# Moving a batch's first output product to the end of its step, and the transposes after it behind the second unit

## The chip, the cores and the metric

The kernel runs on one core of one Trainium2 chip. The metric is the time of the kernel on the device in microseconds (us), the median over runs; less is better. All data is 32-bit float.

## The reference, cut to what matters

```python
def _attn_ref(x, h):                       # x (8, 5696, 128), h (5696, 128)
    L = 2 * S
    Xf, Hf = np.fft.rfft(x, n=L, axis=1), np.fft.rfft(h, n=L, axis=0)
    return np.fft.irfft(Xf * Hf[None], n=L, axis=1)[:, :S, :]

def _moe_ref(x, phi, w1, w2):              # x (45568, 128), 32 slots, 8 experts
    logits = x @ phi
    d = softmax over tokens(logits);  slot_input = d.T @ x
    slot_out = per expert: relu(slot_input @ w1) @ w2
    c = softmax over slots(logits);   return c @ slot_out
```

So a long convolution by Fourier transforms, for 8 batches of 5696 tokens with 128 channels, and behind it a soft mixture of experts over all 45568 tokens.

## The kernel before, in words

The transform is split into small matrix products. **Stage a** (`stage_a`, L230) multiplies folded input by a table (L241), evicts with ScalarE (L243) and stores to the DRAM tensor `f` (L248). It comes in a "low" half once per step and a "high" half once per two steps. **Stage b** works on *units*: a unit loads a tile `gt` of `f` (L270), TensorE multiplies (`stage_b1`, L284) into the single PSUM tile `bt`, VectorE multiplies by the filter's transform (L304 twice, L312 twice) into `yf`, and one unit later `stage_b2` multiplies back (L327), ScalarE evicts (L332) and SyncE stores to `zm` or, for the last third of a batch, to `zr` (queued in `pending`, issued by `flush`). A batch has 12 units; steps of odd number have one, steps of even number two.

**Stage c** works on *pairs* T, four (`NQ`) to a batch, 32 in all. `load_main` and `load_rest` read a pair's `zc` (1 MB, from `zm`) and `zx` (512 KB, from `zr`) into one buffer. `stage_c1` multiplies `zc` (L412) and adds the product of `zx` (L417) in four PSUM banks; ScalarE copies two of them out (L420, L421), VectorE folds (L404, L405, twice each), GpSimd adds (L430, four times). `stage_c2` transposes the result (L439, four groups, each evicted by ScalarE, L441); `stage_c3` multiplies by phi (L448, evicted by L453); `column_max` takes the maximum. In the next odd step `stage_c4` and `stage_c5` transpose logits and weights (L475, L491; evictions L479, L482, L486, L494) and `softmax_exp` runs on VectorE, GpSimd and ScalarE (L500, L501, L504). In the even step after that `softmax_sum` (L509 to L512) and `dispatch` (L527, VectorE L532); `stage_c6` transposes the result (L551, L561, store to `c_t` L562).

The order on each engine is written out by hand in the loop over steps t (L631): what the loop calls first stands first in every engine's queue. PSUM has a ring of four banks (`bank`, L167) that stages a and c take in turn; `bt` and `bz` of stage b have a place of their own, one buffer each. All loads and stores of the loop are issued by SyncE in program order. They use eight semaphores in turn, so that an issue waits until the transfer that had its semaphore eight issues earlier has landed.

Odd steps: stage a low, **c1 of pair T, flush, loads of pair T+1**, unit, c4 of T-1, stage a high, c5 and exp of T-1. Even steps: stage a low, unit, softmax sum and dispatch of T-1, **c2 of T, c6 of T-2**, unit, c3 of T. The `zx` of a batch's first pair holds the product of the batch's last units, which are stored shortly before; its load is issued in the even step ahead of its c1 (`load_rest`, L697), other pairs load `zx` right behind `zc`. From step 72 on stage a has no more work. Behind step 80 the last pairs run without units, then the experts and the output.

Of the kernel before, what the change touches and what calls it, by code (L numbers as in the profile page):

```python
# [70 lines left out]
def kernel(  # L71
# [41 lines left out]
    NQ = NJ // 2  # L113
# [26 lines left out]
    def of_tokens(p):  # L140

        v = p[:, 0:1]
        return bass.AP(tensor=v.tensor, offset=v.offset,
                       ap=[v.ap[0], [TR, 4], [HP, 2], [1, MH]])
# [22 lines left out]
    def bank():  # L167
        rings.append(rings.pop(0))
        return rings[-1].tile([P, 512], F32, name="bank", tag="bank")
# [53 lines left out]
    def flush():  # L223
        while pending:
            pending.pop(0)()
# [140 lines left out]
    def load_main(T):  # L366
        if T >= NT:
            return
        b, j = divmod(T, NQ)
        t_ = zring.pop(0)  # L370
        zring.append(t_)
        zs[T] = t_
        n = 2 * CH
        nc.sync.dma_start(
            out=t_[0][:, :, :, :, :].rearrange("p h n c d -> p (h n c d)"),
            in_=zm[b].rearrange("o k r c d -> (o k) r (c d)")[:, j * n:(j + 1) * n].rearrange(
                "p r x -> p (r x)"))

    def load_rest(T):
        if T >= NT:  # L380
            return
        b, j = divmod(T, NQ)
        t_ = zs[T]
        n = 2 * CH
        nc.sync.dma_start(
            out=t_[1][:, :, :, :].rearrange("p h n d -> p (h n d)"),
            in_=zr[(b + 1) % 2].rearrange("o c k r d -> (o c k) r d")[:, j * n:(j + 1) * n].rearrange(
                "p r x -> p (r x)"))
# [5 lines left out]
    def stage_c1(T, between=lambda: None):  # L394
        zt, zx = zs.pop(T)
        y_ = ybufs.pop(0)
        ybufs.append(y_)

        def part(v, f):
            k = (2 * v + f) * CH  # L400
            return y_[:, k:k + CH, 0:D] if f == 0 else y_[:, k + CH - 1:k - 1:-1, 0:D]

        def fold_out(even, minus, plus):
            nc.vector.tensor_tensor(out=plus, in0=even, in1=minus, op=AL.add)  # L404
            nc.vector.tensor_tensor(out=minus, in0=even, in1=minus, op=AL.subtract)  # L405

        ps = {(o, c): bank() for o, c in ((0, 1), (1, 0), (0, 0), (1, 1))}
        for c in (1, 0):
            for h_ in range(2):
                for o in range(2):  # L410
                    r = slice(o * HP, (o + 1) * HP)
                    nc.tensor.matmul(ps[o, c][h_ * HP:(h_ + 1) * HP, :], im[r, c, :],  # L412
                                     zt[r, h_, :, c, :], start=True, stop=False)
        for h_ in range(2):
            for (o, c), p in ps.items():
                r = slice((2 * o + c) * HALF, (2 * o + c) * HALF + N1 - MAIN)
                nc.tensor.matmul(p[h_ * HP:(h_ + 1) * HP, :], ir[r, :], zx[r, h_, :, :],  # L417
                                 start=False, stop=True)
        ps = {k: p[:, :].rearrange("p (n d) -> p n d", d=D) for k, p in ps.items()}
        nc.scalar.activation(part(0, 0), ps[0, 1], AF.Copy)  # L420
        nc.scalar.activation(om[:, :, :], ps[1, 0], AF.Copy)  # L421
        fold_out(ps[0, 0], part(0, 0), part(1, 0))
        a_ = ps[1, 1]
        between()

        def after():
            fold_out(a_, om[:, :, :], op[:, :, :])
            for v, o_, eng in ((1, op, nc.gpsimd), (0, om, nc.vector if tail else nc.gpsimd)):
                for part_, sign in ((part(v, 1), AL.subtract), (part(v, 0), AL.add)):
                    eng.tensor_tensor(out=part_, in0=part(v, 0), in1=o_[:, :, :], op=sign)  # L430

        ys[T] = y_
        return after

    def stage_c2(T):
        for k in (3, 1, 0, 2) if tail else (3, 2, 1, 0):
            p = bank()
            for i in range(CH):
                nc.tensor.transpose(p[:, i * TR:(i + 1) * TR], ys[T][0:TR, k * CH + i, 0:D],  # L439
                                    ident[0:TR, 0:TR])  # L440
            nc.scalar.activation(yt[:, k * CH:(k + 1) * CH, :, :], of_tokens(p), AF.Copy)  # L441
# [55 lines left out]
    def softmax_exp(T):  # L497
        rm = cpool.tile([P, Q * CH], F32, name="rm", tag="rm", bufs=1)
        Lv = Ls[T][:, :, :, :].rearrange("p k i s -> p (k i) s")
        nc.vector.reduce_max(out=rm[:, :], in_=Lv, axis=AX.X)  # L500
        nc.gpsimd.tensor_tensor(out=Lv, in0=Lv,  # L501
                                in1=rm[:, :].unsqueeze(2).broadcast_to([P, Q * CH, NSL]),
                                op=AL.subtract)
        nc.scalar.activation(Lv, Lv, AF.Exp)  # L504
# [98 lines left out]
    def units(t):  # L603
        g, i = divmod(t - LAG_B, NJ)
        if t < LAG_B or g > B:
            return []
        return [g * NW + k for k in range(sum(PER[:i]), sum(PER[:i + 1]))]
# [23 lines left out]
    for t in range(last_front + 1):  # L631
        us = list(units(t))

        def pair(lag):
            T, half = divmod(t - LAG_C - lag, 2)
            return T if half == 0 and 0 <= T < NT else None

        def prefetch(last):
            nonlocal loaded
            while loaded < len(queue) and queue[loaded][0] <= last \  # L640
                    and queue[loaded][0] // NW * NJ + NJ <= t:
                load_g(queue[loaded][0])
                loaded += 1

        def slot_b(due=True):
            fresh = due and bool(us)
            if fresh:
                u = us.pop(0)
                stage_b1(u)
                prefetch(u + AHEAD)  # L650
                wait_b2.append(u)
            if len(wait_b2) > fresh:
                stage_b2(wait_b2.pop(0))

        T, U, V, W, X = [pair(k) for k in (0, 2, 1, 3, 5)]
        if t < NA:
            stage_a(t, False)
            fold(t + 1)
        if t == last_front:
            assert T is None and U is None  # L660
            assert pair(-1) % NQ
            flush()
            dispatch(W)
            for i in range(3):
                slot_b()
                flush()
                if i == 1:
                    softmax_sum(W)
                    stage_c2(V)
            assert not us and not wait_b2  # L670
            stage_c6(X)
            stage_c3(V)
            column_max(V)
            break
        if t % 2:
            if T is not None:
                stage_c1(T)()
            flush()
            if pair(-2) is not None:
                load_main(pair(-2))  # L680
                if pair(-2) % NQ:
                    load_rest(pair(-2))
            slot_b()
            if U is not None:
                stage_c4(U)
            if t < NA:
                stage_a(t, True)
            if U is not None:
                stage_c5(U)
                softmax_exp(U)  # L690
            flush()
        else:
            if t % NJ == 0:
                prefetch(wait_b2[-1] + AHEAD if wait_b2 else AHEAD - 1)
            if t < NA:
                load_x(t // 2 + 2)
            if pair(-1) is not None and pair(-1) % NQ == 0:  # L697
                load_rest(pair(-1))
            flush()
            slot_b()  # L700
            if W is not None:
                softmax_sum(W)
                dispatch(W)
            flush()
            if V is not None:
                stage_c2(V)
            if X is not None:
                stage_c6(X)
            slot_b()
            if V is not None:  # L710
                stage_c3(V)
                column_max(V)
            flush()
        if t == NA:
            lead.close()
            wts = inner.enter_context(tc.tile_pool(name="wts", bufs=1, side="right"))
            w1s = wts.tile([P, E, F], F32, name="w1s")
        if NA < t <= NA + E:
            nc.sync.dma_start(out=w1s[:, t - NA - 1, :], in_=moe_w1[t - NA - 1])
# [3 lines left out]
    T = V + 1  # L723
# [209 lines left out]
```

## Time and profile before

| | |
|---|---|
| three runs, us | 912.71, 910.75, 908.36; median 910.75 |
| span of the profiled execution, first to last instruction | 906.7 us |
| busy: TensorE (PE) | 757.3 us, 84% |
| busy: VectorE (DVE) / ScalarE (ACT) / GpSimd (POOL) | 601.1 / 436.6 / 399.9 us |
| DMA moved | 278.33 MB, mean 307 GB/s |

The profile gives the span of one execution; its time outside the first and last instruction is not shown, and the median of the runs lies 4.05 us above the span. In the timelines below, the columns are start (us from the span's start), length in us, engine, line, operation, output and inputs, shape, count; in brackets the idle time of the engine just before it and what ended it. PE lengths overlap: the time that a group costs is the distance to the next group's start.

### The profile page before, as it was taken

The numbers are of one execution on the slowest core, as the hardware profiler recorded it, in microseconds if no ns is written. First come the engines' busy times: TensorE is split into PE (matmuls) and PEld (weight loads), VectorE is DVE, ScalarE is ACT, GpSimd is POOL, SyncE is SP. The second block draws the span as 40 slices with busy tenths as digits, with TensorE's granted clock in tenths as the row PEclk, the third lists the DMA queues.
The fourth block names the chain that finished last, engine by engine and source line by source line (L and its number), as shares of the span: only waits on it lengthen the run. The fifth ranks groups of instructions, "written<-read, shape, count | busy, mean of one in ns | idle before, by whom it ended". The sixth has DMA issues, their size and how long they took to land.

```text
span 906.7 us, 21292 instructions
## 1 busy us (share of the span) xinstructions
PE 757.3 (84%) x8308; PEld 383.0 (42%) x8308; DVE 601.1 (66%) x896; ACT 436.6 (48%) x880; POOL 399.9 (44%) x353
## 2 busy tenths in 40 slices
PE   5867687689989998998999999989888877767893
PEld 2222233234444443444444444435444434344882
DVE  2049876567778776777677787758778766653552
ACT  2423343345655565565556555645544444563441
POOL 4634424245656655655555566645332224651000
PEclk9889999989999999999899999989988888766865
DMA  8999999999999999999999999999988868540798
GB/s 264 314 312 342 321 362 290 307 369 357 320 298 375 347 322 337 353 315 291 360 354 331 312 366 348 324 329 331 294 252 293 267 199 341 186 164 1 296 405 332
DMA packets 170443, 278.33 MB, mean 307 GB/s; under 512 B 13543, under 2 KB 128231, under 8 KB 165135
## 3 DMA queue, kind: packets, MB, share of 16 engines
q1 hardware_dynamic: 169336, 275.74, 89.7%
q8 instruction: 66, 1.08, 0.5%
q10 hardware_dynamic: 1008, 1.25, 0.4%
q14 instruction: 33, 0.27, 0.1%
HBM read 147.94 MB, written 129.00 MB: 305 GB/s over the span
## 4 chain that ended last, share of the span: by engine, by line
PE 41%; DMA 32%; DVE 7%; ACT 7%; issue 6%; POOL 3%; SPq 2%; DVEq 0%; ACTq 0%; POOLq 0%
DMA gt<-f 9%; PE bt L284 8%; PE bank L241 7%; PE bz L327 7%; DMA zx<-zr 5%; DMA zc<-zm 5%; PE bank L412 4%; DMA out_dram<-o 4%; DMA f<-fst 4%; PE bank L417 3%; PE bank L439 3%; PE bank L448 2%; DMA zr<-zst 2%; ACT zst L332 2%; ACT fst L243 2%
## 5 line engine op out<-in xcount | busy, mean ns | idle before, releaser
L241 PE MATMUL bank<-x,s 128*32 128x512 f32 (+1 forms) x1152 | 216.5, 613 | 13.3 <-POOL x L217 8.2
L217 POOL TENSOR_TENSOR x<-xc 128x512 f32<-128x512 f32 x144 | 180.5, 1279 | 96.3 <-PE bank L241 77.8
L430 POOL TENSOR_TENSOR y<-y,op 128x512 f32<-128x512 f32 x64 | 77.6, 1212 | 227.6 <-DVE op L404 225.1
L284 PE MATMUL bt<-gt,wt 64*64 64x256 f32 x1620 | 123.3, 414 | 55.2 <-issue 27.1
L243 ACT ACTIVATE fst<-bank 128x512 f32<-128x512 f32 x216 | 123.0, 592 | 77.1 <-PE bank L241 53.5
L304 DVE TENSOR_TENSOR pi<-bt,Hi 128x1024 f32<-128x1024 f32 x96 | 112.9, 1176 | 65.1 <-PE bt L284 65.0
L332 ACT ACTIVATE zst<-bz 128x1024 f32<-128x1024 f32 x96 | 93.3, 972 | 109.8 <-PE bz L327 93.7
L312 DVE TENSOR_TENSOR yf<-bt,pi 128x512 f32<-128x512 f32 x192 | 119.3, 663 | 3.3
L284 PEld LDWEIGHTS bt<-gt,wt 64*64 64x64 f32 x1620 | 57.7, 140 | 135.7 <-issue 77.1
L304 DVE TENSOR_TENSOR bt<-bt,Hr 128x1024 f32<-128x1024 f32 x96 | 113.0, 1177 | 0.0
L327 PE MATMUL bz<-yf,vt 64*64 64x256 f32 x1440 | 109.3, 403 | 0.0
L241 PEld LDWEIGHTS bank<-x,s 128*32 128x32 f32 (+1 forms) x1152 | 54.0, 125 | 129.2 <-issue 91.3
L404 DVE TENSOR_TENSOR y<-bank,y 128x512 f32<-128x512 f32 x32 | 22.1, 692 | 97.2 <-ACT y L420 96.9
L327 PEld LDWEIGHTS bz<-yf,vt 64*64 64x64 f32 x1440 | 63.6, 143 | 25.4 <-issue 4.2
L512 POOL TENSOR_TENSOR L<-L,rs 128x512 f32<-128x512 f32 x32 | 33.5, 1048 | 87.2 <-DVE rs L511 43.7
L439 PE MATMUL bank<-ident,y 109*128 109x109 f32 x512 | 62.6, 272 | 8.8 <-ACT yt L441 8.8
L504 ACT ACTIVATE L<-L 128x512 f32<-128x512 f32 x32 | 20.2, 630 | 102.6 <-POOL L L501 102.6
L430 POOL TENSOR_TENSOR y<-y,om 128x512 f32<-128x512 f32 x54 | 63.9, 1183 | 2.1
L420 ACT ACTIVATE y<-bank 128x512 f32<-128x512 f32 x32 | 19.1, 596 | 93.0 <-PE bank L417 93.0
L439 PEld LDWEIGHTS bank<-ident,y 109*128 109x128 f32 x512 | 52.6, 148 | 20.4 <-POOL x L217 16.4
L412 PE MATMUL bank<-zc,im 64*64 64x512 f32 x480 | 60.8, 623 | 0.0
L441 ACT ACTIVATE yt<-bank 128x360 f32<-128x360 f32 x128 | 53.0, 483 | 6.2 <-PE bank L439 5.8
(101 smaller groups left out, 861.7 us busy)
## 6 DMA issues: line engine op xcount, KB each, us to landing
gt<-f SPq DMA_DIRECT2D x99, 512.0 KB
f<-fst SPq DMA_DIRECT2D x144, 240.0 KB
zm<-zst SPq DMA_DIRECT2D x128, 256.0 KB
zc<-zm SPq DMA_DIRECT2D x30, 1024.0 KB
xc<-in_x_dram SPq DMA_DIRECT2D x32, 768.0 KB
f<-fst SPq DMA_DIRECT2D x144, 120.0 KB
out_dram<-o SPq DMA_DIRECT2D x16, 1024.0 KB
zx<-zr SPq DMA_DIRECT2D x30, 512.0 KB
```

The lines of the kernel that those rows point to most:

```text
L217: nc.gpsimd.tensor_tensor(out=y_[:, o, :, :], in0=near, in1=far, op=AL.subtract if o else AL.add)
L241: nc.tensor.matmul(p[i * m:(i + 1) * m, :], s1[:, g // B, q + o, cols], columns(c_, o), start=True, stop=True)
L243: nc.scalar.activation(st[:, :, q, :], p[:, :].rearrange("p (n d) -> p n d", d=D), AF.Copy)
L284: nc.tensor.matmul(bt[q * HP:(q + 1) * HP, a, o, :], wt[r, 2 * i + q, :], t_[r, 2 * o + q, :, :].rearrange("p c d -> p (c d)"), start=True ...
L304: nc.vector.tensor_tensor(out=p_, in0=pv, in1=h_, op=AL.mult)
L312: nc.vector.tensor_tensor(out=y_[r, 0:k, c, :], in0=pv[:, :, c, :], in1=pi[r, 0:k, 1 - c, :], op=op_)
L327: nc.tensor.matmul(bz[a * HP:(a + 1) * HP, q, o, :], vt[r, i, a, :], y_[r, a * m + o, :, :].rearrange("p c d -> p (c d)"), start=True, sto ...
L332: nc.scalar.activation(st[:, 0:m, 0:n, :].rearrange("p o q x -> p q o x"), bz[:, 0:n, 0:m, :], AF.Copy)
L412: nc.tensor.matmul(ps[o, c][h_ * HP:(h_ + 1) * HP, :], im[r, c, :], zt[r, h_, :, c, :], start=True, stop=False)
L430: eng.tensor_tensor(out=part_, in0=part(v, 0), in1=o_[:, :, :], op=sign)
L439: nc.tensor.transpose(p[:, i * TR:(i + 1) * TR], ys[T][0:TR, k * CH + i, 0:D], ident[0:TR, 0:TR])
L441: nc.scalar.activation(yt[:, k * CH:(k + 1) * CH, :, :], of_tokens(p), AF.Copy)
```

## The change

For the first pair of each batch (T a multiple of 4; pairs 0, 4, ..., 24 fall into the loop over steps), c1, the flush behind it and the loads of the next pair go to the end of the odd step. For the same pairs, c2 and the c6 that stands with it go behind the even step's second unit.

```diff
         if t % 2:
-            if T is not None:
-                stage_c1(T)()
-            flush()
-            if pair(-2) is not None:
-                load_main(pair(-2))
-                if pair(-2) % NQ:
-                    load_rest(pair(-2))
+            late = T is not None and T % NQ == 0
+
+            def begin():
+                if T is not None:
+                    stage_c1(T)()
+                flush()
+                if pair(-2) is not None:
+                    load_main(pair(-2))
+                    if pair(-2) % NQ:
+                        load_rest(pair(-2))
+
+            if late:
+                flush()
+            else:
+                begin()
             slot_b()
             if U is not None:
                 stage_c4(U)
...
                 stage_c5(U)
                 softmax_exp(U)
+            if late:
+                begin()
             flush()
...
             flush()
-            if V is not None:
+            late = V is not None and V % NQ == 0
+            if V is not None and not late:
                 stage_c2(V)
-            if X is not None:
+            if X is not None and not late:
                 stage_c6(X)
             slot_b()
+            if late:
+                stage_c2(V)
+                if X is not None:
+                    stage_c6(X)
             if V is not None:
                 stage_c3(V)
                 column_max(V)
```

## The prediction

> **What bounds the kernel now.** The waits come first: who stood still for whom (total, times, longest, in us).
>
> ```profile
> PEld bank L417 <- DMA zx<-zr: 25.3, 6, 7.4
> PE bank L417 <- DMA zx<-zr: 20.0, 6, 6.5
> ```
>
> TensorE waits six times for `zx`, 20.0 us in all (the first row sees the same waits at the weight loads). By the rows of L417 they stand at pairs 0, 4, 8, 12, 16 and 20: 6.50, 2.27, 2.81, 3.79, 0.69 and 3.92 us; pair 24 waits for nothing. Next the chain that ended last, in the stretch ahead of pair 12's wait (start, us, what):
>
> ```profile
> 417.11 8.31 DMA gt<-f
> 425.43 0.32 SPq L225
> ...
> 426.29 6.58 DMA zx<-zr
> ...
> 432.92 2.01 PE bank L417 x16
> ```
>
> SyncE stood until a `gt` load had landed, because a store needed its semaphore; only then came `zx`, though TensorE had begun that step at 414.41. So the wait is that of a late, full queue. The table by stretches shows how full (length; busy us of PE, PEld, DVE, ACT, POOL; granted clock; DMA share, GB/s):
>
> ```profile
> 262.00:344.00 82.00, 76.27 (x888) 36.57 (x880) 62.54 (x97) 46.83 (x96) 47.07 (x40) 1.00 1.01 341
> 680.00:740.00 60.00, 46.83 (x554) 26.24 (x553) 47.93 (x73) 25.07 (x50) 19.28 (x17) 0.83 0.82 272
> ```
>
> While stage a runs, DMA is busy throughout and TensorE nearly so: two near-equal bounds. Last, the even step behind pair 8, all engines:
>
> ```profile
> 357.08 1.10 PE L284 MATMUL bt<-gt,wt 64*64 64x256 f32 x16 [0.29 <-DVE yf L312]
> 358.00 1.04 PE L327 MATMUL bz<-yf,vt 64*64 64x256 f32 x16
> 358.97 1.09 PE L527 MATMUL bank<-y,d 128*32 128x129 f32 x32
> 360.00 1.34 PE L439 MATMUL bank<-ident,y 109*128 109x109 f32 x12
> 361.80 0.56 PE L439 MATMUL bank<-ident,y 109*128 109x109 f32 x4 [0.47 <-ACT yt L441]
> 362.20 0.54 PE L551 MATMUL bank<-ident,L 109*128 109x109 f32 x4
> 362.67 1.09 PE L284 MATMUL bt<-gt,wt 64*64 64x256 f32 x16
> ```
>
> ```profile
> 358.25 1.22 DVE L304 TENSOR_TENSOR pi<-bt,Hi 128x1024 f32<-128x1024 f32 x1 [0.62 <-PE bt L284]
> ...
> 360.64 1.29 DVE L312 TENSOR_TENSOR yf<-bt,pi 128x512 f32<-128x512 f32 x2
> ```
>
> Between the two units stand 5.6 us (357.08 to 362.67); VectorE needs 4.85 of them (to 361.93) before `bt` is free. The transposes now moved away are the cover of that work.
>
> **What each first pair cost before.** From one L412 to the next pair's: 27.0, 22.5, 23.0, 26.2, 20.9, 26.3 and 20.4 us for pairs 0 to 24. Less its wait, pairs 4, 8 and 16 come to 20.2; pairs 12 and 20 to 22.4, since behind 3.8 and 3.9 us of idleness L417 took 2.01 us, not 1.11, and L284 and L327 were as slow: 2.2 us at a lower clock. Waits of 2.27, 2.81 and, at 171.26, 2.99 left it alone. The Trainium skill (TensorE: Matmul & The Clock Gate, Part 1) says that an idle window of about 3.4 us halves the clock; these rows agree. By that rule the waits added below, 2.0 us at most in a regular pair, cost no clock.
>
> **The odd step.** A is the end of the low product, 344.13 for pair 8, where L412 started. Unit, c4, high product and c5 now come first: 1.89 + 0.59 + 1.85 + 0.59 us (349.94 to 354.86). The unit must wait for VectorE, whose unit before ends at 344.49: **+0.4**, new, because c1 no longer stands between. Then L412, 1.9. L417 comes at A + 7.2 instead of A + 1.9; `zx` landed at A + 2.5 to A + 5.8 for pairs 4 to 20, so the five waits go. Pair 0 has no c4 and c5: L417 could start at 181.7, `zx` lands at 183.4, 1.7 remain. In c1, TensorE waits for the second low eviction before; afterwards for c5's (L494 ends 1.3 after c5 starts), the same within 0.1. The exponential L504 now stands ahead of L420, but its GpSimd step L501 no longer stands behind L430; it ends at about A + 7.7, L420 starts at A + 8.3: nothing.
>
> **The even step.** The low product needs the bank that L420 empties (350.06 + 0.60, TensorE free at 349.94): **+0.75**; this eviction lay beside the unit before. The folds (L404, L405, 2.8 us) lie beside the low product and end before the first unit's L304 is due. First unit, back product and dispatch take 0.92 + 0.97 + 1.03 = 2.9 us; the second unit needs `bt`, free 4.85 behind the first one's start: **+2.0**. The y that c2 needs is ready: L430 ends 4.8 us behind the second fold, earlier than c2's new place. Behind c2 there is only c6 to cover ScalarE: the eviction L332 (1.03) and four L441 (1.70) end 2.75 us behind c2's start, c2 and c6 take 1.8 + 0.47: c3 waits **+0.5**. The waits of 0.29 and 0.47 above go. Sum 0.4 + 0.75 + 2.0 + 0.5 - 0.76 = **+2.9**, and a first pair costs 20.2 + 2.9 = 23.1 us. Nothing of it hides: TensorE's idle time in these stretches is these waits.
>
> **Pair 24** runs without stage a. Its unit waits 2.2 us for VectorE, its second even unit about 4.3, since the folds come right ahead of the first unit's multiplications; a wait of 2.28 goes. That makes +2.3 at full clock, +4.3 at the lower one that these steps showed before; I take +3.
>
> **TensorE's sum**, pairs 0 to 24: to 24.4 (-2.6), +0.6, +0.1, -3.1, +2.2, -3.2, +3.0: -3.0 us.
>
> **The loads of the next pair.** `zc` and `zx` of T+1 now stand behind a `gt` load, two `zm` stores and four `f` stores in SyncE's queue. In a pair whose c1 came on time:
>
> ```profile
> 457.10 0.52 SPq L374 DMA_DIRECT2D zc<-zm  x1
> 457.79 0.80 SPq L385 DMA_DIRECT2D zx<-zr  x1
> 458.68 0.43 SPq L270 DMA_DIRECT2D gt<-f  x1
> 459.77 1.79 SPq L225 DMA_DIRECT2D zm<-zst  x2
> 461.66 3.61 SPq L225 DMA_DIRECT2D f<-fst  x4
> 467.59 0.34 SPq L198 DMA_DIRECT2D xc<-in_x_dram  x1
> ```
>
> The seven took 8.9 us (458.68 to 467.59), part of it waiting for landings; their 1.5 MB are 4.5 us at 334 GB/s. No row shows the order itself, so `zc` comes 4.5 to 8.9 us later; I take 6, near the 6.6 to the last store's end. `zc` of pairs 1, 5, 9, 13, 17 and 21 landed 6.7, 6.1, 5.9, 8.4, 6.1 and 9.6 us before its L412 (landing: last update of the load's semaphore). With the pair lengths changed as above, 4.1, 6.7, 6.0, 5.3, 8.3 and 6.4 remain: a delay of 6 leaves waits of 1.9 and 0.7, **+2.6**; 4.5 leaves 0.4, 8.9 leaves 16.6. `zx` follows 1.3 us behind `zc` and is wanted 1.9 later: nothing. The next input load waits behind both, but its fold is not due for a step.
>
> **Sum**: -3.0 + 2.6 = -0.4 us on a span of 906.7; with the 4.05 us between span and median, **910.4 us**. A measurement can tell about 0.5%, 4.55 us, from no change.
>
> **Rivals.**
>
> *DMA sets the batch* (no change, 910.7). `zx` landed at 183.4, 265.8, 348.8, 432.9, 515.9 and 600.1: 82.4 to 84.1 us apart, whatever TensorE lost in between, and the DMA share is 1.00. Then the moved product doesn't free the loop: TensorE runs ahead until `zc` stops it. With landings kept and `zc` 6 us later, L412 of pair 21 comes 3.1 us earlier than before, pair 24 gives 3 back. Against it: SyncE also stood for compute, 12.5 us in 10 waits for L284. The Trainium skill (DMA: Bandwidth & Descriptors, Specifications) puts a core's share of HBM at about 358 GB/s, close above the 341 here, which would speak for this rival; but slices of this trace reach 405, so it is no ceiling here.
>
> *The later loads decide* (slower). If `zc` comes 8.9 us later and DMA has no lead to give, the waits at six L412 are 16.6: +13.6 us, 924.4. It decides from a delay of about 7.3 (8.0 us of waits, +5.0). For it: the seven issues did take 8.9. Against: two of those waits were for `zc` and `zx` themselves.
>
> *Half the price* (faster). If the second unit's wait and c3's come to half, because evictions and VectorE's order fit better than rows of another order show, 1.25 us go from each of seven pairs: -9.2 us, 901.6. Against: the 4.85 us of VectorE have stood behind every unit.
>
> **Chances.** Forecast 0.50, DMA 0.17, later loads 0.20, half price 0.13. So faster 0.13, within 0.5% 0.67, slower 0.20. The range: downwards no `zc` waits and pair 24 at +2.3 (907.1), and part of the half price: 905; upwards the forecast with `zc` about 8.0 later (11.5 us of waits, +8.5): 919. That leaves out the ends of the two outer rivals.
>
> **What would show it.** L417 of pairs 4 to 20 without a wait for `zx`, pair 0 with under 2 us; L284 of the even step behind waiting about 2 us for L312, L448 about 0.5 for L441, the low L241 about 0.75 for L420; L327 to L439 adjacent; no 1112 ns matmuls at pairs 12 and 20; L412 of pairs 1 and 13 waiting a little for `zc`. A wait over 2 us at most of the L412 behind would prove the second rival, `zx` waits at the new place the first, second-unit waits under 1 us the third.

## The result and the profile after

The changed kernel takes 918.08 us (median of 7 runs, 914.73 to 919.38), the kernel before, run beside it, 912.03: a ratio of 1.0064, 95% interval 1.0037 to 1.0091. It is slower, by about 6 us, where 0.4 us less was forecast. Measured once more on another chip, beside 26 runs of the kernel before (908.98), it gave 914.64 and 1.0069 (1.0042 to 1.0096). The ratios leave out the runs that lie over 1.5% above the fastest of their kernel; the medians hold all runs.

The profiled execution has a span of 917.6 us and took 919.38, so 1.8 us lie around the span. The kernel before's profiled span of 906.7 therefore belongs to a run of about 908.4, below its median of 912.03: the two spans, 10.9 us apart, overstate the change. 1.6 us of that are there before step 27, ahead of the first edit.

The waits of TensorE for the loads of stage c, whole execution; the first two rows are those shown of the kernel before:

```profile
PEld bank L417 <- DMA zx<-zr: 14.1, 9, 3.6
PE bank L417 <- DMA zx<-zr: 5.9, 6, 2.7
...
PE bank L412 <- DMA zc<-zm: 0.5, 2, 0.3
```

From 20.0 us the waits at L417 fell to 5.9 (pairs 0, 12, 16, 20: 2.70, 1.21, 0.71, 0.78; the rest at 9 and 13). So the change takes away most of these waits. The even step behind pair 8, where the price was to lie, with TensorE's low product ahead of it:

```profile
357.31 1.94 PE L241 MATMUL bank<-x,s 128*64 128x512 f32 x8 [0.79 <-ACT y L420]
359.18 1.09 PE L284 MATMUL bt<-gt,wt 64*64 64x256 f32 x16
360.10 1.04 PE L327 MATMUL bz<-yf,vt 64*64 64x256 f32 x16
361.07 1.09 PE L527 MATMUL bank<-y,d 128*32 128x129 f32 x32
364.13 1.09 PE L284 MATMUL bt<-gt,wt 64*64 64x256 f32 x16 [1.97 <-issue]
365.02 1.07 PE L327 MATMUL bz<-yf,vt 64*64 64x256 f32 x16
366.02 1.71 PE L439 MATMUL bank<-ident,y 109*128 109x109 f32 x16
367.58 0.59 PE L551 MATMUL bank<-ident,L 109*128 109x109 f32 x4
368.67 0.81 PE L448 MATMUL bank<-yt,phi 128*32 128x360 f32 x8 [0.50 <-ACT yt L441]
```

Three new waits: 0.79 for ScalarE's eviction, 1.97 ahead of the second unit, 0.50 ahead of c3. The second is marked "issue", but VectorE's row shows whose it is: its two L312 start at 362.74 and take 1.29, to 364.03. A fourth, 0.38, stands ahead of the odd step's unit at 348.39. The bracketed waits of 0.29 and 0.47 of before are gone.

The stretches and the chain ahead of pair 12's wait, as shown of before:

```profile
262.00:344.00 82.00, 75.92 (x860) 37.33 (x860) 61.93 (x95) 46.73 (x96) 44.62 (x39) 0.98 0.98 327
680.00:740.00 60.00, 45.26 (x572) 26.45 (x564) 45.32 (x70) 25.73 (x53) 18.89 (x17) 0.87 0.81 268
```

```profile
423.65 8.05 DMA gt<-f
431.72 0.32 SPq L225
...
432.57 7.90 DMA zx<-zr
...
440.51 1.19 PE bank L417 x16
```

In the first stretch the granted clock is 0.98, where it was 1.00, and DMA moves 327 GB/s, not 341. The chain is the same one, 6.3 to 6.5 us later, and its `zx` load takes 7.90 us instead of 6.58. The queue behind pair 8's product, in the new order:

```profile
359.33 0.38 SPq L270 DMA_DIRECT2D gt<-f  x1
359.98 1.54 SPq L225 DMA_DIRECT2D zm<-zst  x2
361.81 2.48 SPq L225 DMA_DIRECT2D f<-fst  x4
364.40 0.35 SPq L374 DMA_DIRECT2D zc<-zm  x1
365.72 0.35 SPq L385 DMA_DIRECT2D zx<-zr  x1
```

The seven issues ahead of `zc` took 5.1 us (359.33 to 364.40); `zc` landed at 371.34, and L412 started at 371.48.

The measure for what follows is the length of a *batch*: from L412 of pairs 1, 5, 9, 13, 17 and 21, whose place the change leaves alone, to the L412 four pairs on, in each profile (us):

| kernel | 1 | 5 | 9 | 13 | 17 | 21 | sum |
|---|---|---|---|---|---|---|---|
| before | 82.1 | 83.0 | 86.2 | 80.9 | 86.3 | 79.7 | 498.2 |
| changed | 84.0 | 83.6 | 85.3 | 84.9 | 84.3 | 83.7 | 505.8 |
| changed, second chip (after_same) | 84.0 | 83.2 | 84.4 | 83.2 | 84.6 | 85.9 | 505.3 |
| forecast by TensorE's sum | 82.7 | 83.1 | 83.1 | 83.1 | 83.1 | 82.7 | 497.8 |

The last row is the prediction's 23.1 us for the first pair (20.36 + 3 for pair 24), and for the other three pairs what they took before (59.6, four times 60.0, 59.37).

### The profile page after: what moved, and what is told of

It reads as the page before. It is cut to its first block, busy times and chain, and to the rows that moved or that the text cites. A ratio compares the mean times of both kernels' runs of the same rounds, so it can differ in the third digit from the quotient of the medians.

```text
span 917.6 us, 21233 instructions
## 1 busy us (share of the span) xinstructions
PE 751.2 (82%) x8308; PEld 381.8 (42%) x8308; DVE 604.9 (66%) x896; ACT 438.5 (48%) x880; POOL 399.7 (44%) x353
## 4 chain that ended last, share of the span: by engine, by line
PE 39%; DMA 32%; issue 8%; ACT 8%; DVE 6%; POOL 5%; SPq 1%; ACTq 0%; DVEq 0%; POOLq 0%
DMA gt<-f 10%; DMA zx<-zr 10%; PE bank L241 8%; PE bt L284 8%; PE bz L327 6%; PE bank L412 4%; DMA out_dram<-o 4%; DMA f<-fst 3%; PE bank L417 3%; POOL y L430 3%; PE bank L439 2%; PE bank L448 2%; ACT fst L243 2%; DMA zc<-zm 2%; ACT zst L332 2%
## 5 line engine op out<-in xcount | busy, mean ns | idle before, releaser
L241 PE MATMUL bank<-x,s 128*32 128x512 f32 (+1 forms) x1152 | 218.0, 616 | 19.8 <-POOL x L217 8.2
L284 PE MATMUL bt<-gt,wt 64*64 64x256 f32 x1620 | 121.7, 409 | 71.5 <-issue 41.8
L312 DVE TENSOR_TENSOR yf<-bt,pi 128x512 f32<-128x512 f32 x192 | 119.4, 663 | 3.3
L284 PEld LDWEIGHTS bt<-gt,wt 64*64 64x64 f32 x1620 | 58.3, 139 | 150.9 <-issue 79.0
L241 PEld LDWEIGHTS bank<-x,s 128*32 128x32 f32 (+1 forms) x1152 | 55.5, 125 | 138.2 <-issue 97.8
L412 PE MATMUL bank<-zc,im 64*64 64x512 f32 x480 | 60.6, 618 | 0.6 <-DMA zc<-zm 0.5
L501 POOL TENSOR_TENSOR L<-L,rm 128x512 f32<-128x512 f32 x32 | 33.6, 1049 | 55.0 <-DVE rm L500 54.0
```

The costliest lines, as they stand in the source:

```text
L241: nc.tensor.matmul(p[i * m:(i + 1) * m, :], s1[:, g // B, q + o, cols], columns(c_, o), start=True, stop=True)
L284: nc.tensor.matmul(bt[q * HP:(q + 1) * HP, a, o, :], wt[r, 2 * i + q, :], t_[r, 2 * o + q, :, :].rearrange("p c d -> p (c d)"), start=True ...
L312: nc.vector.tensor_tensor(out=y_[r, 0:k, c, :], in0=pv[:, :, c, :], in1=pi[r, 0:k, 1 - c, :], op=op_)
```

## The experiments

Ratios are to the kernel before, run beside the variant on the same chip, with 95% intervals. The kernel before itself lies between 907 and 912 us from chip to chip, so ratios or batches are compared, not medians of different chips.

**One half of the change at a time.** The edit is `late = False` in the even step (c1_only) or in the odd step (c2_only).

> First part alone: c1 and the next pair's loads of a first pair at the end of the odd step, c2 and c6 at their old place. TensorE's own price per first pair by rows of the changed kernel: 0.4 (unit behind VectorE) + 0.75 (low product behind L420) + about 0.4 (c2's last group behind L430) - 0.3 = 1.25 us, not 2.9. Theory 'TensorE's own sum' (what the product is moved past costs, and zx lands early enough): 7 x 1.65 = 11.5 us faster than the changed kernel, about 906, with no zx wait. Theory 'DMA sets the pace' (the loads of zx land every 84 us whatever TensorE does): 2 to 5 us faster than the changed kernel, 911 to 916, with zx waits of 1 to 2 us back at the moved L417.

> Second part alone: c1 as before, c2 and c6 of a first pair behind the second unit. TensorE's own price per first pair: 2.0 (second unit behind VectorE) + 0.5 (c3 behind L441) - 0.76 = 1.7 us. 'TensorE's own sum': 7 x 1.7 = 12 us slower than before, about 924, with the zx waits of the kernel before (20 us in all) unchanged. 'DMA sets the pace': the next zx wait gives the 1.7 us back, so that only the first pairs without a wait pay: +2 to +5 us, 914 to 917, and the zx waits fall to some 10 us.

c1_only: 911.48 us, 1.0024 (0.9991 to 1.0057), no clear difference, where TensorE's own sum had expected a gain of some 5 us. Its waits of over 0.4 us for `zx` fell to pairs 1, 9 and 20, but `zc` of pairs 5, 9, 13, 17 and 21 came late by 1.55, 0.45, 1.13, 1.56 and 1.27 us. c2_only: 922.16 us, 1.0146 (1.0098 to 1.0194), as TensorE's own sum had it:

```profile
PE bank L417 <- DMA zx<-zr: 14.8, 6, 4.0
```

Its `zx` waits fell by only 5 us (from 20.0), so the added work was not given back at the next wait. The second part is the costly one.

**The price without DMA in the way.** In `load_x` each row's length becomes a quarter; these kernels leave out three quarters of the input's columns:

```diff
-                                ap=[v.ap[0], [(a[1] - a[0]) * D, 2], [1, n * D]])
+                                ap=[v.ap[0], [(a[1] - a[0]) * D, 2], [1, n * D // 4]])
                     nc.sync.dma_start(
-                        out=t_[r0:r1, :, :, :].rearrange("p s n d -> p s (n d)"), in_=v)
+                        out=t_[r0:r1, :, 0:n // 4, :].rearrange("p s n d -> p s (n d)"), in_=v)
```

> The kernel before with only a quarter of each input load (x is left out for three quarters of the columns, which stay zero), 18 MB less of 278; all else in place. 'DMA sets the pace': 2.3 MB less a batch are 6.9 us at 334 GB/s, so zx comes in time, its waits fall under 5 us in all and a batch to TensorE's own 80.2 us: 15 to 22 us faster than before, 890 to 897. 'TensorE's own sum' with a zx whose lateness is the latency of store and load behind the last unit: waits stay above 10 us, 3 to 8 us faster.

> The changed kernel with the same quarter of each input load. No zx or zc wait is left, so the price on TensorE stands alone: 'DMA sets the pace' expects 15 to 20 us above before_light (7 x 2.9, less what zx waits were left there), 908 to 914. 'TensorE's own sum' expects 3 to 8 us above before_light, as with full loads.

> c1_only with the quarter input loads of the light kernels (x is left out for three quarters of the columns): no DMA wait is left, so the price of the first part stands alone. TensorE's own sum: 1.25 us for each of six pairs, some 2 for pair 24, against before_light's 883.7: 892 to 895; so 11 to 14 us below after_light's 905.9, which is the price of moving c2 and c6. If the price lies in the moved c1 instead, c1_light is within 5 us of after_light.

before_light: 883.65 us, 0.9716 (0.9674 to 0.9758). Its waits:

```profile
PE bank L417 <- DMA zx<-zr: 2.2, 3, 1.0
```

c1_light: 889.57, 0.9760 (0.9716 to 0.9805). after_light: 905.88, 0.9982 (0.9956 to 1.0008), with no `zx` or `zc` wait of over 0.1 us (c1_light has one, 0.94 for `zc` at pair 13). before_light and after_light ran on one chip: where hardly a load is late the change costs 22.2 us, against 20.3 (7 x 2.9) by the sum. c1_light ran on another, so the split is rougher: by the medians 5.9 us are the first part's and 16.3 the second's, by the ratios (of 907.37) 4.0 and 20.1, by the sums of the six batches (480.4, 490.9, 505.0) 10.5 and 14.1. Each way the second part is the larger.

Both light kernels lie beyond what 'DMA sets the pace' expected (before_light 24 us below the kernel before, not 15 to 22; after_light 22 above before_light, not 15 to 20), and far from the 3 to 8 us of the other theory. So in the kernel before it is the volume of the loads that makes `zx` late; what the moved work costs is TensorE's own, as in c2_only, where the added time was not given back.

The batches of after_light are 84.0, 83.1, 84.5, 84.4, 83.2 and 85.8; the first five of c1_light lie between 81.2 and 82.5, those of before_light between 79.8 and 81.2. Two of after_light's first five are as forecast, the other three 1.3 to 1.4 longer, and the last is 3 us longer. That pointed at the clock.

**The clock.** Three products of 128x64 by 128x512 without a reader stand in the wait ahead of the second unit:

```diff
+            if late and t < NA:
+                p = bank()
+                for _ in range(3):
+                    nc.tensor.matmul(p[0:HP, :], ident[:, 0:HP],
+                                     wt[:, 0:8, :].rearrange("p n r -> p (n r)"),
+                                     start=True, stop=True)
             slot_b()
```

> after_light with three extra products of 128x64 by 128x512 (about 0.47 us each; their result is not read) in the even step of pairs 0 to 20, in the wait ahead of the second unit; x is left out for three quarters of the columns as in after_light. If the 2.0 us of idleness there is what lowers the clock behind it in some pairs (1.3 us each in three of five batches of after_light), the granted clock stays at 1 there, all batches from pair 1 to pair 21 take 83.1 us instead of 83.1 to 84.5, and the time falls by 3 to 5 us from after_light's 905.9. If idleness there is not the cause, the extra products change nothing or cost up to 1.4 us a pair.

904.63 us, 0.9931 (0.9904 to 0.9958). Batches 83.7, 83.8, 83.8, 83.9, 83.8: the long ones are gone and all are alike, but the three products take 2.7 us, 0.7 more than the wait, so that the batches are no shorter on average. By times this would settle little (medians 905.88 and 904.63 of two chips, ranges overlapping); the rows do.

**The order of the loads.** In before_zx_first and after_zx_first, `load_rest` of the even step stands ahead of `load_x`. In before_zr_zx_first, also the 1 MB load of `zc` of a first pair stands behind its step's unit and the flush that stores `zr`. In after_loads_first, `begin` issues the loads ahead of the stores:

```diff
                 if T is not None:
                     stage_c1(T)()
-                flush()
+                if not late:
+                    flush()
                 if pair(-2) is not None:
                     load_main(pair(-2))
```

> The kernel before with the load of a first pair's zx ahead of the input load in the even step, not behind it. If the place in SyncE's queue and the 768 KB ahead of it make zx late, it lands about 2 us earlier (768 KB at 334 GB/s are 2.3 us): zx waits 20 to about 8 us, no low clock behind them, 8 to 12 us faster, 900 to 904. If DMA as a whole sets the pace, the input load lands that much later and the wait moves to other loads: within 3 us of before.

> As before_zx_first, and in the odd step ahead of it the stores of the batch's last unit (zr) stand ahead of the 1 MB load of zc, not behind it, so that zx need not wait for them. Queue order: zx lands some 4 us earlier, no wait for it, but zc comes 2 us later than its slack of 4 to 6 us: 15 us faster, about 897. DMA as a whole: within 4 us of before.

> The changed kernel with zx ahead of the input load. Its remaining zx waits (5.5 us in all) go: 3 to 6 us faster than the changed kernel, 912 to 915. If DMA as a whole sets the pace, the time stays that of the changed kernel, 918, and gt or zc waits take their place.

> The changed kernel with the next pair's loads ahead of the six stores that the end of the odd step issues. zc of pairs 9, 13, 17 and 21 lands 3 to 5 us earlier and their waits (1.7 us in all) go: 1 to 2 us faster than the changed kernel, if the later stores delay nothing. If DMA as a whole sets the pace: no change, 918, zx of the next batch waits longer instead. If SyncE, which now has to wait for c1 ahead of the stores, is what matters: 3 us or more slower.

before_zx_first: 911.33, 1.0028 (0.9997 to 1.0059): nothing gained. L417's waits for `zx` fell to 16.2 us, but units now waited 13.3 us for `gt`, where it had been 6.1:

```profile
PE bt L284 <- DMA gt<-f: 13.3, 8, 4.5
```

before_zr_zx_first: 904.44, 0.9941 (0.9904 to 0.9978), faster, though less than by queue order alone. after_zx_first: 919.98, 1.0104 (1.0056 to 1.0152). (No trace reading rests on these two.) after_loads_first: 916.17, 1.0094 (1.0063 to 1.0125). In its trace no `zc` or `zx` wait is left but pair 0's 2.33 us, and batches are 84.0, 83.1, 84.4, 83.1, 84.4 and 83.5: the loads are in time, and the loss is not smaller.

**All on one chip.** The changed kernel again; its variant with loads first (loads_same); that with two extra products (loads_warm); and the first part alone, for pairs 0 to 20, loads first (c1_loads_same, run before as c1_loads_first).

> The changed kernel once more, beside the three below on one chip. Waits for zx and zc of some 7 us in all at the first pairs and the pairs behind them; batches of 83.5 to 85.3 us; slower than before by 5 to 9 us.

> after_loads_first once more: the changed kernel with the next pair's loads ahead of the six stores. No wait for zx or zc but at pair 0. If the waits that came back are what costs: 5 us or more below after_same. If TensorE's own longer pairs and the lowered clock are: within 3 us of after_same, batches of 83.1 or 84.4 us.

> loads_same with two extra products (their result is not read) in the wait ahead of the second even unit of pairs 0 to 20. If the lowered clock is part of the price, no batch of pairs 1 to 21 is above 83.6 us and the time falls 2 to 4 us below loads_same; what then stays above before is TensorE's own price. If not, as loads_same.

> Full loads, reference's output. The first part alone, for pairs 0 to 20 alone (pair 24 as before), with the next pair's loads ahead of the end of step's six stores. TensorE's own sum: 20.2 + 1.25 = 21.5 us for a first pair against 22.5 to 26.3 before, so 8 to 13 us faster than before, 895 to 900, if DMA can follow at 81.5 us a batch. If DMA cannot follow below some 83 us a batch, the waits come back at zx and zc and the time is within 3 us of before.

> c1_loads_first once more: first part alone, pairs 0 to 20, loads ahead of the stores. TensorE's price 1.25 us a first pair, not 2.9: 10 to 16 us below after_same, 5 to 10 us below before.

after_same 914.64, 1.0069 (1.0042 to 1.0096). loads_same 916.46, 1.0082 (1.0050 to 1.0114). loads_warm 912.20, 1.0030 (1.0007 to 1.0053). In after_same's trace no L412 or L417 of a first pair or the pair behind waited for DMA; its batches stand in the table above. The waits expected of it were not there, yet it is as slow as the first time. So the loss does not need the waits for loads. The batches of loads_same are 82.8, 84.7, 84.4, 83.2, 84.5 and 86.1; loads_warm's are 82.8, 83.1, 83.2, 83.1, 83.2 and 86.3, the forecast to 0.1 us in the first five. loads_warm's pair 4:

```profile
277.13 1.09 PE L527 MATMUL bank<-y,d 128*32 128x129 f32 x32
278.15 1.93 PE L724 MATMUL bank<-wt,ident 128*64 128x512 f32 x4
280.19 1.09 PE L284 MATMUL bt<-gt,wt 64*64 64x256 f32 x16
281.08 1.07 PE L327 MATMUL bz<-yf,vt 64*64 64x256 f32 x16
282.08 1.71 PE L439 MATMUL bank<-ident,y 109*128 109x109 f32 x16
```

and the same place in the changed kernel, with the table by stretches of that step and of pair 8's (length, then busy us of PE, PEld, DVE, ACT, POOL; granted clock; DMA share, GB/s):

```profile
279.52 1.09 PE L284 MATMUL bt<-gt,wt 64*64 64x256 f32 x16 [1.97 <-issue]
280.41 1.62 PE L327 MATMUL bz<-yf,vt 64*64 64x256 f32 x16
281.96 2.78 PE L439 MATMUL bank<-ident,y 109*128 109x109 f32 x16
```

```profile
276.00:285.00 9.00, 7.03 (x96) 5.32 (x88) 8.73 (x12) 3.48 (x6) 8.92 (x8) 0.81 0.94 327
360.00:369.00 9.00, 6.54 (x113) 4.70 (x108) 8.52 (x12) 3.86 (x7) 8.84 (x9) 1.00 1.06 386
```

The unit starts at full speed behind the wait, then the clock falls: 1.62 and 2.78 us instead of 1.07 and 1.71, at a granted clock of 0.81. With the wait filled, it doesn't. L448's wait (0.19 instead of 0.50) takes a part back, so that 1.3 us remain.

Why pair 4 and not pair 8, with the same wait of 1.97? In every trace the granted clock changes only at multiples of 3.41 us from its first change. The changed kernel's profile is cut at these places here, in two stretches around each of the two waits (idle time is the length less PE's busy time):

```profile
277.39:280.80 3.41, 1.44 (x32) 1.14 (x28) 3.34 (x5) 0.23 (x1) 3.33 (x4) 1.00 1.02 339
280.80:284.22 3.42, 3.42 (x28) 2.59 (x20) 3.35 (x7) 1.86 (x3) 3.42 (x4) 0.50 0.89 323
359.32:362.73 3.41, 2.84 (x64) 1.81 (x62) 2.99 (x3) 1.59 (x2) 3.33 (x3) 1.00 1.06 381
362.73:366.14 3.41, 2.01 (x33) 1.45 (x34) 3.33 (x7) 0.00 (x0) 3.33 (x4) 1.00 1.09 384
```

At pair 4 the whole wait lies in one stretch, where TensorE is idle for 1.97 of 3.41 us, and the next runs at 0.50. At pair 8 it is split, 0.57 and 1.40, and the clock stays. The three waits of before that kept the clock (2.27, 2.81, 2.99) were split as well, with at most 1.82 us in one stretch; a wait of 2.99 in after_same, at pair 0, lay in one, and L284 behind it took 1.94 us instead of 1.09. Over all 17 traces, from 165 to 740 us, a stretch at full clock with less than 1.3 us of idleness was never followed by a low one (1719 stretches), one with more than 2.0 us always (107), and 43 of the 115 between were. The border is not sharp: pair 4 of loads_same has its 1.97 us in one stretch, and the clock stayed; the idle time is that of TensorE's records, of which a few can be missing.

c1_loads_first, the version that beats both: 902.70, 0.9900 (0.9864 to 0.9936) on one chip, 903.67, 0.9947 (0.9915 to 0.9979) on the other. Batches 81.1, 82.5, 82.5, 82.1, 85.2, 80.0. With c2 in its old place the wait ahead of the second unit does not arise; instead c2's last group waits a little for GpSimd:

```profile
357.00 1.45 PE L439 MATMUL bank<-ident,y 109*128 109x109 f32 x12
359.12 0.59 PE L439 MATMUL bank<-ident,y 109*128 109x109 f32 x4 [0.67 <-POOL y L430]
359.55 0.54 PE L551 MATMUL bank<-ident,L 109*128 109x109 f32 x4
360.02 1.09 PE L284 MATMUL bt<-gt,wt 64*64 64x256 f32 x16
```

## Why the prediction was wrong

**What held.** The waits of a regular first pair came out nearly as priced: 0.38, 0.79, 1.97 and 0.50 us for 0.4, 0.75, 2.0 and 0.5, the old 0.29 and 0.47 gone. A batch without a drop of the clock takes 83.1 us, as forecast (after_same, after_light, after_loads_first), against 80.2 of before without waits (before_light, 80.2 in its cleanest batch). The five waits for `zx` shrank from 13.5 to 2.8 us in one execution of the change and to nothing in the other.

**The step that failed first: "By that rule the waits added below, 2.0 us at most in a regular pair, cost no clock."** They did. The wait of 1.97 lowered the clock behind it in pair 4 of the changed kernel's trace and in three of five batches of after_same, at 1.3 to 1.5 us each (granted clock 0.96 in 40 us around each of the three, 1.00 around the two others); with it filled, loads_warm has none and its ratio falls from 1.0069 or 1.0082 to 1.0030. I took the three waits of before that kept the clock (2.27, 2.81, 2.99) as a bound; each of them was split over two stretches of 3.41 us. The Trainium skill (TensorE: Matmul & The Clock Gate, Part 1) has the deciding window of about 3.4 us run freely. The traces agree: the stretches are 3.41 us long, and one and the same wait lowers the clock in three of five batches; but a drop behind 1.97 us of idleness is not what I read out of its "idle window".

**The second: pair 24, "I take +3".** The batch that holds it grew from 79.7 to 83.7 and, in after_same, 85.9: +4.0 and +6.2. The second unit's wait was 4.2, as worked out (4.3), but in the longer one the clock was low ahead of it too, behind two waits of 2.25 and 1.71 for VectorE and ScalarE. TensorE's rows there, in after_same:

```profile
690.16 3.51 PE L412 MATMUL bank<-zc,im 64*64 64x512 f32 x16
693.60 1.18 PE L417 MATMUL bank<-zx,ir 26*64 26x512 f32 x16
...
696.60 1.09 PE L527 MATMUL bank<-y,d 128*32 128x129 f32 x32
701.93 1.98 PE L284 MATMUL bt<-gt,wt 64*64 64x256 f32 x16 [4.23 <-issue]
703.66 1.96 PE L327 MATMUL bz<-yf,vt 64*64 64x256 f32 x16
705.55 2.63 PE L439 MATMUL bank<-ident,y 109*128 109x109 f32 x16
```

L412 took 3.51 us, not 1.95. Half clock at L412 was in neither of my two bounds, +2.3 and +4.3.

Together these are the miss in after_same: its batches lie 7.5 us above the forecast row of the table, 1.3 + 0.1 + 1.3 + 0.1 + 1.5 = 4.3 in the first five, nearly all by the clock, and 3.2 by pair 24. In the first profile of the change nearly the same excess, 8.0 us, has other parts: 1.3 by the clock at pair 4, 1.0 by pair 24, and most of the rest by loads that were still late, 2.8 us of waits for `zx` at pairs 8 to 20, which the prediction said would go, and 2.0 us by which `zc` and `zx` lengthened pairs 9, 13 and 17, where it had 2.6. The waits on TensorE were priced rightly; TensorE's sum was too small by the clock and by pair 24.

**The rest of the sum.** Pair 0 gained nothing: it still waited 2.70 us for `zx`, not 1.7, the clock fell behind it (the low L241 took 3.33 us instead of 1.94), and the second unit waited 3.00, not 2.0. The delay of `zc` was about 5 us, not 6. No run shows the lead that would have given pair 0 its 2.6 us.

**The rivals.** "DMA sets the batch" had no change and waits for `zx` at the new place; after_same has none of these waits and is slower, so DMA does not set the changed kernel's batch. As a floor it is not refuted: in c1_loads_first and c1_loads_same waits for `zx` of 0.6 to 1.6 us came back, and the first five batches of each average 82.7 us, inside the 82.4 to 84.1 that I took for DMA's pace. And the loads do make `zx` late: with 18 MB less of them, 24 us of the kernel before vanish. That the landings of `zx` were evenly spaced before may also mean that they follow TensorE's last unit; no run tells the two apart. "The later loads decide" gave the right sign for a wrong reason: after_loads_first takes its cause away and is no faster. "Half the price" is refuted by the rows.

What stays open: which of the profiled drops of the clock the median run has; it lies between one and three in five batches.

## What to carry to other kernels

A step that is moved out of a wait's way must be priced by what it covered where it stood: here the transposes were the only cover of VectorE's work on a single PSUM buffer, and moving them cost 14 to 20 us, while the product alone could be moved for 4 to 10. A wait of about 2 us on TensorE is to be priced at a lowered clock as well, as a chance: here 1.3 us more each time that it fell into one stretch of 3.41 us. An even rhythm of landings and a DMA share of 1.00 leave open whether the loads set the pace; a kernel with a part of the bytes taken out tells more (the waits for `zx` fell from 20.0 to 2.2 us).

## What the runs showed of the hardware

A wait of 1.97 us lowered the granted clock (0.50 for 3.41 us, 0.81 over 9 us) in some executions and steps and not in others, while 2.81 and 2.99 us had not in the kernel before. What told them apart was how much idleness fell into one stretch of a fixed rhythm of 3.41 us: 1.97 at pair 4, 0.57 and 1.40 at pair 8. TensorE work that nobody reads, put into such a wait, kept the clock at 1.00 in all five batches of loads_warm. A DMA share of 1.00 is not its upper end: it was 0.98 at 327 GB/s and 1.01 at 341 over 82 us, and 1.06 at 386 over 9.
